# Moving the last subtraction of sixteen weight conversions from GpSimd to VectorE, and one conversion to the next step

## The chip, the cores and the metric

One core of a Trainium2 chip runs the whole program. Its engines work in parallel, each through its own queue in a fixed order: TensorE (PE in the profile; PEld is its weight load), VectorE (DVE), ScalarE (ACT), GpSimd (POOL) and SyncE (SP, which only issues transfers here). An instruction whose input is not ready holds back all that stand behind it on its engine. The metric is the device time of one execution, in microseconds; lower is better.

## The reference

Three layers follow one another: a decaying linear attention (2 batches, 8 heads, 768 positions, head size 64), a dense feed-forward layer with a gate, and a mixture of 8 experts of which each token takes one.

```python
x = attn_out.transpose(0, 2, 1, 3).reshape(B * S, H * D)          # 1536 x 512
h = x @ w_in                                                      # 512 x 2048
sp = np.where(h > 20.0, h, np.log1p(np.exp(np.minimum(h, 20.0))))
x = (h * np.tanh(sp)) @ w_out                                     # 2048 x 512
e_idx = np.argmax(x @ w_gate + modality_bias[modality_id], axis=1)
out[mask] = gate_w[mask, None] * (np.maximum(x[mask] @ w1[e], 0.0) @ w2[e])
```

`w_in` and `w_out` arrive as 64-bit floats. The kernel reads them as pairs of 32-bit words and makes of each weight a high and a low 32-bit part, so that a product is formed of three matmuls.

## The kernel before

The dense layer is cut into 16 blocks of 128 hidden columns (`fc`), and the 1536 tokens into 4 chunks of 384 (`c`). The list `order` (lines 865 and 866) sets the passes: first blocks 0 to 7 for chunks 0, 1 and 2, then blocks 8 to 15 for the same chunks, then all 16 blocks for chunk 3. A pass of the loop at line 867 is called a step here, and its number is `i`. Each step does four things:

- The first nine steps (0 to 8) carry the end of the attention (`attend`).
- `convert_next` takes one or two weight blocks from the list `wq`: it starts the transfer of the raw words (line 294 for `w_in`, 303 for `w_out`) and queues the conversion. There are 32 conversions; `stg["n"]` counts them. The first 16 are taken by step 5, the other 16 from step 9 on.
- `mm1` makes 12 matmuls for the step (line 804, into a PSUM tile `w`, of which there are three) and the gate: ScalarE line 809 (Exp), VectorE 810, ScalarE 811, 812, 813, VectorE 814, 815, 816, ScalarE 817, VectorE line 103 (`mg<-me,mg`). Line 816 is the last reader of the PSUM tile, so `mm1` of step i + 3 cannot start before line 816 of step i has ended.
- `mm2a` makes 9 matmuls (line 830) of the step three before, into three accumulators `a`, of which there are three. After blocks 0 to 7 of a chunk, `put_by` copies the accumulators out (ScalarE, line 386, into two halves of a tile `cv` and a tile `xq`) and writes them to DRAM (line 387). That is at steps 10, 18 and 26. The next chunk needs the three accumulators free.

A conversion (`convert`) is a chain over three engines: ScalarE 278 and 279, VectorE 280 and 281, ScalarE 282 (the high part), and GpSimd line 103 (the low part, `wo<-cv,wo` or `wi<-cv,wi`). Line 103 is the body of the helper `tt`, so it stands for many elementwise operations; the tile names tell them apart. From step 9 the raw words lie mostly in tile `cv`, which has two buffers in turn; a buffer is free when the low part of its conversion has been made. `put_by` takes its `cv` from the same two buffers.

The order of instructions on each engine is not that of the code: a scheduler in the build sorts them by its own estimate of when each is ready, and the order is then fixed.

Of the kernel before, what the change touches and what calls it, by code (L numbers as in the profile page):

```python
# [7 lines left out]
F32 = mybir.dt.float32  # L8
# [5 lines left out]
ALU = mybir.AluOpType  # L14
# [13 lines left out]
FA = 8  # L28
# [4 lines left out]
def tile_decay_attention_mish_moe_top1(  # L33
# [66 lines left out]
    V, A, G = nc.vector, nc.scalar, nc.gpsimd  # L100

    def tt(o, a, b, op, eng=None):
        (eng or V).tensor_tensor(out=o, in0=a, in1=b, op=op)  # L103
# [32 lines left out]
    n = 1  # L136
# [138 lines left out]
    def convert(raw, hi, lo):  # L275
        H_, L_ = raw[:, :, 1], raw[:, :, 0]
        hf = H_.bitcast(F32)
        A.activation(out=hf, in_=hf, func=AF.Copy, scale=REBIAS)  # L278
        A.activation(out=L_, in_=raw.rearrange("p f w -> p (f w)").bitcast(U8)[:, 3::8], func=AF.Copy, scale=2.0 ** -5, bias=2.0 ** -6 - 0.5)
        V.scalar_tensor_tensor(out=L_, in0=H_, scalar=-0x80000000, in1=L_, op0=ALU.bitwise_and, op1=ALU.bitwise_or)  # L280
        V.scalar_tensor_tensor(out=H_, in0=H_, scalar=3, in1=L_, op0=ALU.logical_shift_left, op1=ALU.bitwise_or)  # L281
        A.activation(out=hi, in_=hf, func=AF.Copy)
        tt(lo, hf, hi.bitcast(F32), ALU.subtract, G)

    stg = {"tags": ["cv", "cv"], "n": 0}

# [5 lines left out]
    def load_wi(fc):  # L292
        s = raw_tile()
        nc.sync.dma_start(out=s.rearrange("p (a f) w -> p a (f w)", a=KC),
                          in_=w_in[:, fc * 2 * P:(fc + 1) * 2 * P].rearrange("(a p) f -> p a f", p=P))
        t = T([P, 2, KC, P], F32R, f"wi{fc}")
        tf = t.rearrange("p h a f -> p h (a f)")
        convert(s, tf[:, 0], tf[:, 1])
        wi[fc] = t

    def load_wo(fc):
        s = raw_tile()
        nc.sync.dma_start(out=s.rearrange("p f w -> p (f w)"), in_=w_out[fc * P:(fc + 1) * P, :])
        t = T([P, 2, DM], F32R, f"wo{fc}")
        convert(s, t[:, 0], t[:, 1])
        wo[fc] = t
# [4 lines left out]
    def convert_next(n, limit=NFC):  # L311
        for _ in range(n):
            ok = [w for w in wq if w[2] < limit]
            if ok:
                wq.remove(ok[0])
                _, kind, f = ok[0]
                (load_wi if kind == "i" else load_wo)(f)
# [446 lines left out]
    def early(which, fc):  # L764
        if which == 1:
            if fc == 8:
                E2["R1"] = [T([P, FF], F32, f"wi{j}") for j in range(4)]
                E2["er"] = nc.sync.value_load(E2["e0"][0:1, 0:1], min_val=0, max_val=NE - 1)
                load_raw(E2["er"], 1)
            if 10 <= fc < 14:  # L770
                j = fc - 10
                E2["W1h"].append(T([P, FF], F32R, f"wi{4 + j}"))
                E2["W1l"].append(T([P, FF], F32R, f"wi{8 + j}"))
                split(E2["W1h"][j], E2["W1l"][j], E2["R1"][j])
            if fc == 14:
                E2["XTh"] = T([P, KC, 256], F32R, "wi12")
                E2["XTl"] = T([P, KC, 256], F32R, "wi13")
                prep_x(gather(E2["u"][0], (0, 1), NE1 * P), 2)
        else:
            if fc == 5:  # L780
                E2["R2"] = [T([P, 2, DM], F32, f"wo{j}") for j in range(4)]
                load_raw(E2["er"], 2)
            if 10 <= fc < 14:
                j = fc - 10
                E2["W2h"].append(T([P, 2, DM], F32R, f"wo{4 + j}"))
                E2["W2l"].append(T([P, 2, DM], F32R, f"wo{8 + j}"))
                split(E2["W2h"][j], E2["W2l"][j], E2["R2"][j])
# [3 lines left out]
    def step():  # L791
        if steps:
            f = steps.pop(0)
            if f is not None:
                f()

    def mm1(c, fc):
        ph = PS([P, CW], "w")
        n = 0
        for kk in range(KC):  # L800
            wh, wl = wi[fc][:, 0, kk, :], wi[fc][:, 1, kk, :]
            xh, xl = xth[c][:, kk, :], xtl[c][:, kk, :]
            for a_, b_ in ((wh, xh), (wh, xl), (wl, xh)):
                nc.tensor.matmul(ph, lhsT=a_, rhs=b_, start=(n == 0), stop=(n == 3 * KC - 1))  # L804
                n += 1
        ex = T([P, CW], F32, "me", 3)
        gg = T([P, 2, CW], F32R, "mg", 4)
        rr = T([P, CW], F32, "mr", 1)
        A.activation(out=ex, in_=ph, func=AF.Exp)  # L809
        V.tensor_scalar(out=ex, in0=ex, scalar1=EXP20, scalar2=None, op0=ALU.min)  # L810
        A.activation(out=ex, in_=ex, func=AF.Square, bias=one[:, 0:1])  # L811
        A.activation(out=rr, in_=ex, func=AF.Ln, bias=one[:, 0:1])  # L812
        A.activation(out=gg[:, 1], in_=rr, func=AF.Exp, scale=-1.0)  # L813
        V.scalar_tensor_tensor(out=ex, in0=ex, scalar=1.0, in1=gg[:, 1].bitcast(F32), op0=ALU.add, op1=ALU.mult)  # L814
        V.scalar_tensor_tensor(out=ex, in0=ex, scalar=-2.0, in1=gg[:, 1].bitcast(F32), op0=ALU.add, op1=ALU.mult)  # L815
        V.scalar_tensor_tensor(out=ex, in0=ex, scalar=0.5, in1=ph, op0=ALU.add, op1=ALU.mult)  # L816
        A.activation(out=gg[:, 0], in_=ex, func=AF.Copy)  # L817
        tt(gg[:, 1], ex, gg[:, 0].bitcast(F32), ALU.subtract)
        gs[c, fc] = gg

    def mm2a(c, fc):
        divided_at = FA if c < NCK - 1 else NFC
        if fc in (0, divided_at):
            accs[c] = [PS([P, DM], "a") for _ in range(CT)]
        gg = gs.pop((c, fc))
        wh, wl = wo[fc][:, 0], wo[fc][:, 1]
        for j in range(CT):
            gh, gl = gg[:, 0, j * P:(j + 1) * P], gg[:, 1, j * P:(j + 1) * P]
            for i, (a_, b_) in enumerate(((gh, wh), (gh, wl), (gl, wh))):
                nc.tensor.matmul(accs[c][j], lhsT=a_, rhs=b_, start=(fc in (0, divided_at) and i == 0),  # L830
                                 stop=(fc in (divided_at - 1, NFC - 1) and i == 2))
        if fc == divided_at - 1 < NFC - 1:
            put_by(c, accs.pop(c))
        if c < NCK - 1 and fc == NFC - 3:
            fetch(c)
        if c == NCK - 1:
            early(2, fc)
        if fc == NFC - 1:
            steps.extend(route(c, accs.pop(c)))
            if c == NCK - 2:  # L840
                steps.extend([stage1, stage1b, None, stage1c, lambda: slots(0, NE1)])

    def attend(it):
        if it + 2 < NIT:
            keys(it + 2)
        if it + 2 < NIT:
            queries(it + 2)
        if it + 3 < NIT:
            load_q(it + 3)
        if it == 0:  # L850
            decay(1, s1)
        elif it + 1 < NIT:
            decay(it + 1, scores(it + 1))
        if it + 3 < NIT:
            load_k(it + 3)
        combine(it)
        if it + 2 < NIT:
            load_v(it + 2)
# [8 lines left out]
    for i, (c, fc) in enumerate(order):  # L867
        it = CT + i
        if it < NIT:
            if it == NIT - CT:  # L870
                stg["tags"] = ["cv", "cv", "wi10"]
            attend(it)
            convert_next(2, FA)
        else:
            if it == NIT:
                stg["tags"] = ["cv", "wo14", "cv", "wo15"]
            if wq and wq[0][2] >= 13:
                stg["tags"] = ["cv", "cv"]
            convert_next(2 if i < FA + 1 or i % 3 == 0 else 1)
        mm1(c, fc)  # L880
        step()
        if c == NCK - 1:
            early(1, fc)
        if i >= LAG:
            mm2a(*order[i - LAG])
        step()
# [317 lines left out]
```

## Time and profile before

| | |
|---|---|
| median of three runs | 574.85 us (574.23 to 575.75) |
| profiled execution, its own time | 574.69 us |
| span of its instructions | 573.0 us |
| TensorE busy | 528.6 us (92%) |
| VectorE busy | 343.6 us (60%) |
| ScalarE busy | 302.3 us (53%) |
| GpSimd busy | 117.5 us (21%) |
| mean granted TensorE clock | 0.980 of full speed |

In the rows of the profile a timeline entry gives start, duration, engine, line, operation and tiles, and in brackets how long the engine stood idle before it and what ended the idle time. A table by stretch gives the stretch, its length, then busy time and count of TensorE matmul, TensorE weight load, VectorE, ScalarE and GpSimd, then the granted TensorE clock, the share of the transfer engines and GB/s. A row of a group gives the count, busy time in us, mean ns of one, and after the bar the idle time before them with its releasers. All starts are us from the start of the span.

### The profile page before, as it was taken

What the parts mean: (1) busy time and instruction counts of PE and PEld (TensorE: products, weight loads), DVE (VectorE), ACT (ScalarE), POOL (GpSimd) and SP (SyncE); (2) the same over time, 40 slices, a digit from 0 to 9 for tenths busy, and PEclk for the clock granted to TensorE, in tenths of its full rate; (3) what the DMA queues carried; (4) which work ended last, traced back from release to release, by engine and by line L of the source; (5) the groups of instructions that cost most, each with busy time, mean ns of one, the idle gap of its engine ahead of it and who ended that gap; (6) DMA issues with size and microseconds to landing.
All of it is one profiled execution on the core that took longest, in us unless ns stands there. A gap on an engine that the chain in (4) does not pass through costs nothing.

```text
span 573.0 us, 10275 instructions
## 1 busy us (share of the span) xinstructions
PE 528.6 (92%) x3577; PEld 457.7 (80%) x3578; DVE 343.6 (60%) x814; ACT 302.3 (53%) x580; POOL 117.5 (21%) x100
## 2 busy tenths in 40 slices
PE   7898989989979999999999999999788998998993
PEld 4687768778768889999998999989677887778882
DVE  3579989788887656766767599947512024503020
ACT  2457867778887766656566479632111124412120
POOL 1654453423321000000000003000502212312111
PEclk9999989999989999999999999999888999999998
DMA  8999565323342020011030046001469427402120
GB/s 161 235 249 266 139 151 148 112 92 112 110 128 112 19 92 1 0 44 67 1 94 17 2 152 234 2 0 57 116 226 350 149 58 254 156 28 69 49 59 34
DMA packets 67371, 62.24 MB, mean 109 GB/s; under 512 B 42183, under 2 KB 51919, under 8 KB 67280
## 3 DMA queue, kind: packets, MB, share of 16 engines
q1 hardware_dynamic: 62064, 51.65, 30.5%
q0 software_dynamic: 2976, 9.44, 5.5%
q8 instruction: 44, 0.72, 0.5%
q10 hardware_dynamic: 2240, 0.05, 0.2%
q14 instruction: 47, 0.39, 0.2%
HBM read 52.47 MB, written 8.86 MB: 107 GB/s over the span
## 4 chain that ended last, share of the span: by engine, by line
PE 41%; DMA 24%; issue 14%; DVE 7%; ACT 7%; POOL 5%; SPq 1%; POOLq 0%; DVEq 0%; ACTq 0%
PE a L830 16%; PE w L804 15%; DMA out_dram<-cv,xth 9%; DMA out_dram<-xth,xth 9%; DMA cv<-in_moe_w_out_dram 3%; POOL wo L103 3%; PE a L571 2%; PE w L581 2%; PE r L433 2%; DMA cv<-in_moe_w_in_dram 2%; POOL wi L103 1%; DVE cv L280 1%; DVE cv L281 1%; ACT cv L278 1%; DMA out_dram<-mg,xth 1%
## 5 line engine op out<-in xcount | busy, mean ns | idle before, releaser
L830 PE MATMUL a<-wo,mg 128*128 128x512 f32 x576 | 148.3, 399 | 5.4 <-ACT cv L386 2.8
L804 PE MATMUL w<-xth,wi 128*128 128x384 f32 x512 | 146.1, 345 | 3.6 <-DVE me L816 3.1
L830 PEld LDWEIGHTS a<-wo,mg 128*128 128x128 f32 x576 | 106.7, 189 | 27.5 <-ACT cv L386 4.0
L804 PEld LDWEIGHTS w<-xth,wi 128*128 128x128 f32 x512 | 94.5, 189 | 10.1 <-DVE me L816 5.7
L804 PE MATMUL w<-xtl,wi 128*128 128x384 f32 x256 | 86.8, 339 | 0.0
L581 PE MATMUL w<-wi,wi 128*128 128x256 f32 x576 | 75.4, 290 | 9.5 <-issue 7.6
L581 PEld LDWEIGHTS w<-wi,wi 128*128 128x128 f32 x576 | 72.9, 195 | 11.7 <-issue 9.0
L585 DVE SCALAR_TENSOR_TENSOR wo<-w,wi 128x256 fp32r<-128x256 f32 x48 | 20.2, 424 | 84.1 <-ACT wi L584 76.8
L571 PE MATMUL a<-wo,wi 128*128 128x512 f32 x192 | 62.5, 407 | 4.5 <-ACTq L1143 3.0
L814 DVE SCALAR_TENSOR_TENSOR me<-me,mg 128x384 f32<-128x384 f32 x64 | 41.5, 649 | 31.0 <-ACT mg L813 30.8
L804 PEld LDWEIGHTS w<-xtl,wi 128*128 128x128 f32 x256 | 48.6, 190 | 1.7
L584 ACT ACTIVATE wi<-w 128x256 fp32r<-128x256 f32 x48 | 18.2, 384 | 58.7 <-PE w L581 58.7
L817 ACT ACTIVATE mg<-me 128x384 fp32r<-128x384 f32 x64 | 33.3, 520 | 28.2 <-DVE me L816 27.8
L809 ACT ACTIVATE me<-w 128x384 f32<-128x384 f32 x64 | 31.0, 485 | 30.5 <-PE w L804 30.0
L571 PEld LDWEIGHTS a<-wo,wi 128*128 128x128 f32 x192 | 35.7, 192 | 13.7 <-issue 6.2
L811 ACT ACTIVATE me<-me,one 128x384 f32<-128x384 f32 x64 | 39.0, 609 | 12.0 <-DVE me L810 11.7
L103 DVE TENSOR_TENSOR mg<-me,mg 128x384 fp32r<-128x384 f32 x64 | 36.6, 573 | 10.6 <-ACT mg L817 10.2
L812 ACT ACTIVATE mr<-me,one 128x384 f32<-128x384 f32 x64 | 39.3, 613 | 1.2
L815 DVE SCALAR_TENSOR_TENSOR me<-me,mg 128x384 f32<-128x384 f32 x64 | 38.5, 602 | 1.1
L571 PE MATMUL a<-wo,wo 128*128 128x512 f32 x96 | 38.6, 402 | 0.0
L816 DVE SCALAR_TENSOR_TENSOR me<-me,w 128x384 f32<-128x384 f32 x64 | 35.2, 551 | 1.5
L103 POOL TENSOR_TENSOR xtl<-xtl,id 128x1152 f32<-128x1152 f32 x1 | 2.1, 2116 | 156.5 <-DVE xtl L103 156.5
(269 smaller groups left out, 724.7 us busy)
## 6 DMA issues: line engine op xcount, KB each, us to landing
xtl<-in_moe_w_dram SPq DMA_DIRECT2D x24, 256.0 KB
cv<-in_moe_w_out_dram SPq DMA_DIRECT2D x11, 512.0 KB
cv<-in_moe_w_in_dram SPq DMA_DIRECT2D x9, 512.0 KB
wi<-in_moe_w_dram SPq DMA_DIRECT2D x8, 512.0 KB
wo<-in_moe_w_dram SPq DMA_DIRECT2D x8, 512.0 KB
wo<-in_k_dram SPq DMA_DIRECT2D x12, 256.0 KB
wi<-in_q_dram SPq DMA_DIRECT2D x12, 256.0 KB
wo<-in_v_dram SPq DMA_DIRECT2D x12, 256.0 KB
```

The costliest lines, as they stand in the source:

```text
L103: (eng or V).tensor_tensor(out=o, in0=a, in1=b, op=op)
L571: nc.tensor.matmul(po, lhsT=a_, rhs=b_, start=(f == 0 and i == 0), stop=(f == FC2 - 1 and i == 2))
L581: nc.tensor.matmul(ph, lhsT=a_, rhs=b_, start=(n == 0), stop=(n == 3 * KC - 1))
L804: nc.tensor.matmul(ph, lhsT=a_, rhs=b_, start=(n == 0), stop=(n == 3 * KC - 1))
L809: A.activation(out=ex, in_=ph, func=AF.Exp)
L811: A.activation(out=ex, in_=ex, func=AF.Square, bias=one[:, 0:1])
L812: A.activation(out=rr, in_=ex, func=AF.Ln, bias=one[:, 0:1])
L814: V.scalar_tensor_tensor(out=ex, in0=ex, scalar=1.0, in1=gg[:, 1].bitcast(F32), op0=ALU.add, op1=ALU.mult)
L815: V.scalar_tensor_tensor(out=ex, in0=ex, scalar=-2.0, in1=gg[:, 1].bitcast(F32), op0=ALU.add, op1=ALU.mult)
L816: V.scalar_tensor_tensor(out=ex, in0=ex, scalar=0.5, in1=ph, op0=ALU.add, op1=ALU.mult)
L817: A.activation(out=gg[:, 0], in_=ex, func=AF.Copy)
L830: nc.tensor.matmul(accs[c][j], lhsT=a_, rhs=b_, start=(fc in (0, divided_at) and i == 0), stop=(fc in (divided_at - 1, NFC - 1) and i == 2))
```

## The change

`tt` gets its engine from the count of conversions: the first 16 keep GpSimd, the last 16 use VectorE. And of the steps whose number divides by three only those under 16 take two conversions.

```diff
         A.activation(out=hi, in_=hf, func=AF.Copy)
-        tt(lo, hf, hi.bitcast(F32), ALU.subtract, G)
+        tt(lo, hf, hi.bitcast(F32), ALU.subtract, G if stg["n"] <= 2 * FA else V)
...
-            convert_next(2 if i < FA + 1 or i % 3 == 0 else 1)
+            convert_next(2 if i < FA + 1 or (i % 3 == 0 and i < 2 * FA) else 1)
```

Step 18 is the first of them. There `convert_next` took blocks 12 and 13 of `w_out`, then block 14 at step 19 and block 15 at step 20; now it takes block 12 at step 18, 13 at 19, 14 at 20 and 15 at 21.

On VectorE, at the conversion of block 11 of `w_out` (raw words `cv_1650`, low part `wo11_1652`), with the gate of step 15 (`me_1628`), of step 16 (`me_1672`) and of step 17 (`me_1716`):

```order
+L103 TENSOR_TENSOR wi14_1608<-cv_1606,wi14_1608 128x512 [waits Activation_49]
 L815 SCALAR_TENSOR_TENSOR me_1628<-me_1628,mg_1629 128x384 [waits DVE_49]
-L810 TENSOR_SCALAR me_1672<-me_1672 128x384 [waits Activation_49]
+L280 SCALAR_TENSOR_TENSOR cv_1650<-cv_1650 128x512 [waits DMAHW2_49,Activation_49]
 L816 SCALAR_TENSOR_TENSOR me_1628<-me_1628,w_1615 128x384 [waits DVE_49]
-L280 SCALAR_TENSOR_TENSOR cv_1650<-cv_1650 128x512 [waits DMAHW2_49,Activation_49,Pool_49]
 L281 SCALAR_TENSOR_TENSOR cv_1650<-cv_1650 128x512 [waits DVE_49]
+L810 TENSOR_SCALAR me_1672<-me_1672 128x384
 L103 TENSOR_TENSOR mg_1629<-me_1628,mg_1629 128x384 [waits PE_49,Activation_49]
+L810 TENSOR_SCALAR me_1716<-me_1716 128x384
+L103 TENSOR_TENSOR wo11_1652<-cv_1650,wo11_1652 128x512 [waits Activation_49]
 L814 SCALAR_TENSOR_TENSOR me_1672<-me_1672,mg_1673 128x384 [waits Activation_49]
```

The low parts now stand among the gates, line 810 of step 16 stands behind lines 280 and 281 of the raw words instead of ahead of them, and line 810 of step 17 stands ahead of line 814 of step 16.

On ScalarE, at the write-out of chunk 1 (`put_by` at step 18), before the change; `cv_1747` holds the raw words of block 13 of `w_out`, `cv_1791` and `xq_1792` are the tiles of the write-out, `me_1769` is the gate of step 18:

```order
L386 ACTIVATE xq_1792<-a_1446 128x512 [waits DMAHW5_49,PE_49]
L811 ACTIVATE me_1769<-me_1769,one_169 128x384 [waits DVE_49]
L812 ACTIVATE mr_1771<-me_1769,one_169 128x384 [waits Activation_49]
L282 ACTIVATE wo12_1740<-cv_1738 128x512 [waits DVE_49]
L813 ACTIVATE mg_1770<-mr_1771 128x384 [waits Activation_49]
L278 ACTIVATE cv_1747<-cv_1747 128x512 [waits DMAHW5_49,Pool_49]
L279 ACTIVATE cv_1747<-cv_1747 128x512
L386 ACTIVATE cv_1791<-a_1444 128x512 [waits Pool_49]
L386 ACTIVATE cv_1791<-a_1445 128x512
```

The same place after the change, where the gate of step 18 is `me_1760` and the tiles of the write-out are `cv_1782` and `xq_1783`:

```order
L386 ACTIVATE xq_1783<-a_1446 128x512 [waits DMAHW5_49,PE_49]
L278 ACTIVATE cv_1738<-cv_1738 128x512 [waits DMAHW4_49,DVE_49]
L282 ACTIVATE wi15_1696<-cv_1694 128x512 [waits DVE_49]
L817 ACTIVATE mg_1673<-me_1672 128x384 [waits DVE_49]
L279 ACTIVATE cv_1738<-cv_1738 128x512
L811 ACTIVATE me_1760<-me_1760,one_169 128x384 [waits DVE_49]
L386 ACTIVATE cv_1782<-a_1444 128x512 [waits DVE_49]
L812 ACTIVATE mr_1762<-me_1760,one_169 128x384 [waits Activation_49]
L386 ACTIVATE cv_1782<-a_1445 128x512
```

The copies into `cv` waited for the low part of block 12 of `w_out` and stood behind lines 278 and 279 of block 13; now they wait for the low part of block 15 of `w_in`, one conversion earlier in the turn of the two buffers, and block 13 comes after them.

On SyncE, at the same place, before the change (`cv_1747` and `cv_1799` are blocks 13 and 14 of `w_out`):

```order
L303 DMA cv_1738<-in_moe_w_out_dram 128x1024 [waits DMAHW2_49,Pool_49]
L303 DMA cv_1747<-in_moe_w_out_dram 128x1024 [waits DMAHW5_49,DMAHW3_49,Pool_49]
L387 DMA part_231<-xq_1792 128x512 [waits Activation_49]
L387 DMA part_231<-cv_1791 128x512 [waits Activation_49] x2
L303 DMA cv_1799<-in_moe_w_out_dram 128x1024 [waits DMAHW5_49,Pool_49]
```

And after it (`cv_1790` and `cv_1837` are blocks 13 and 14):

```order
L303 DMA cv_1738<-in_moe_w_out_dram 128x1024 [waits DMAHW2_49,DVE_49]
L387 DMA part_231<-xq_1783 128x512 [waits DMAHW5_49,Activation_49]
L387 DMA part_231<-cv_1782 128x512 [waits Activation_49] x2
L303 DMA cv_1790<-in_moe_w_out_dram 128x1024 [waits DMAHW4_49,DVE_49]
L303 DMA cv_1837<-in_moe_w_out_dram 128x1024 [waits DMAHW7_49,DMAHW6_49,DMAHW3_49]
```

The transfer of block 13 moves behind the three writes of the write-out. Every transfer of raw words waited for GpSimd's low part of the buffer's last user and now waits for VectorE's. On GpSimd 16 rows go and none comes; its next work after the attention is then a single row, at 344.76 us in the trace of before.

## Rows read from the trace of the kernel before

**Rows 1.** Table by stretch, core 0, 112 to 190 us and within it.

```profile
112.00:190.00 78.00, 69.28 (x327) 59.16 (x326) 63.06 (x104) 63.92 (x125) 22.73 (x16) 0.98 0.33 108
...
130.00:165.00 35.00, 32.43 (x160) 27.96 (x158) 30.04 (x51) 29.86 (x58) 11.19 (x7) 1.00 0.35 112
```

**Rows 2.** Timeline of TensorE, 110 to 192 us: groups that waited.

```profile
114.90 0.44 PE L804 MATMUL w<-xth,wi 128*128 128x384 f32 x1 [0.29 <-DVE xtl L103]
...
128.19 1.87 PE L830 MATMUL a<-wo,mg 128*128 128x512 f32 x6 [1.58 <-ACT cv L386]
...
157.26 0.44 PE L804 MATMUL w<-xth,wi 128*128 128x384 f32 x1 [1.18 <-DVE me L816]
...
167.35 1.18 PE L830 MATMUL a<-wo,mg 128*128 128x512 f32 x3 [2.54 <-ACT xq L386]
...
168.32 0.52 PE L804 MATMUL w<-xth,wi 128*128 128x384 f32 x1
...
172.67 1.64 PE L830 MATMUL a<-wo,mg 128*128 128x512 f32 x6 [1.26 <-ACT cv L386]
...
190.11 0.44 PE L804 MATMUL w<-xth,wi 128*128 128x384 f32 x1 [0.76 <-DVE me L816]
```

**Rows 3.** Chain that ended last, two of its undisturbed TensorE pieces.

```profile
194.54 2.10 PE w L804 x12
...
236.62 2.09 PE w L804 x12
```

**Rows 4.** Table by stretch again, 168 to 170 us.

```profile
168.00:170.00 2.00, 2.00 (x8) 1.90 (x7) 0.76 (x3) 1.91 (x4) 0.39 (x1) 0.50 0.71 186
```

**Rows 5.** Timeline of VectorE and GpSimd, 119 to 123 us.

```profile
119.16 3.07 POOL L103 TENSOR_TENSOR wi<-wo,wi 128x512 fp32r<-128x512 f32 x2 [5.33 <-ACT wi L282]
...
119.53 1.52 DVE L814 SCALAR_TENSOR_TENSOR me<-me,mg 128x384 f32<-128x384 f32 x1
120.98 1.47 DVE L810 TENSOR_SCALAR me<-me 128x384 f32<-128x384 f32 x1
```

**Rows 6.** Groups of VectorE instructions, shapes apart, 112 to 190 us.

```profile
L814 DVE SCALAR_TENSOR_TENSOR me<-me,mg 128x384 f32<-128x384 f32 x16 | 12.4, 777 | 7.2 <-ACT mg L813 7.1
...
L810 DVE TENSOR_SCALAR me<-me 128x384 f32<-128x384 f32 x15 | 10.1, 673 | 0.9 <-ACT me L809 0.9
...
L815 DVE SCALAR_TENSOR_TENSOR me<-me,mg 128x384 f32<-128x384 f32 x15 | 9.4, 629 | 0.3
...
L816 DVE SCALAR_TENSOR_TENSOR me<-me,w 128x384 f32<-128x384 f32 x15 | 8.2, 549 | 0.3
```

**Rows 7.** The same groups where GpSimd is silent, 200 to 236 us.

```profile
L814 DVE SCALAR_TENSOR_TENSOR me<-me,mg 128x384 f32<-128x384 f32 x9 | 5.0, 559 | 11.1 <-ACT mg L813 11.1
...
L816 DVE SCALAR_TENSOR_TENSOR me<-me,w 128x384 f32<-128x384 f32 x9 | 5.0, 554 | 0.3
...
L810 DVE TENSOR_SCALAR me<-me 128x384 f32<-128x384 f32 x9 | 3.2, 352 | 0.0
```

**Rows 8.** Instructions on tile cv, 107 to 200 us: duration min/median/max.

```profile
L281 DVE SCALAR_TENSOR_TENSOR cv<-cv x13: 680/685/695, 109.8 to 185.2; 128x512 int32<-128x512 int32 x13
...
L103 POOL TENSOR_TENSOR wo<-cv,wo x8: 1306/1360/1862, 134.5 to 186.9; 128x512 fp32r<-128x512 f32 x8
```

**Rows 9.** Groups of ScalarE instructions, shapes apart, 112 to 190 us.

```profile
L811 ACT ACTIVATE me<-me,one 128x384 f32<-128x384 f32 x15 | 9.2, 611 | 6.8 <-DVE me L810 6.8
...
L278 ACT ACTIVATE cv<-cv 128x512 f32<-128x512 f32 x11 | 7.4, 677 | 4.3 <-DMA cv<-in_moe_w_out_dram 2.7 <-POOL wo L103 1.0 <-DMA cv<-in_moe_w_in_dram 0.7
...
L282 ACT ACTIVATE wo<-cv 128x512 fp32r<-128x512 f32 x8 | 5.4, 671 | 0.4 <-DVE cv L281 0.3
```

**Rows 10.** Timeline of ScalarE around the second write-out of accumulators.

```profile
170.91 0.69 ACT L278 ACTIVATE cv<-cv 128x512 f32<-128x512 f32 x1 [0.96 <-POOL wo L103]
...
172.04 1.05 ACT L386 ACTIVATE cv<-a 128x512 f32<-128x512 f32 x2
```

**Rows 11.** Chain that ended last: one load of raw weights.

```profile
152.22 3.32 DMA cv<-in_moe_w_out_dram
```

## The prediction

> **What bounds the kernel now.** The page puts TensorE first, so I asked where it stands still. The table by stretch shows it busy for 69.28 of the 78 us from 112 to 190 [rows 1]: the steps that carry the last 16 conversions. The timeline of TensorE then shows what ended each wait [rows 2]: twice ScalarE's copies of accumulators (1.58 us, then 2.54 and 1.26 in one write-out), and several times VectorE's line 816, which gives the PSUM tile of three steps earlier back (1.18, 0.76). TensorE also loses time at half speed. After the 2.54 us wait the granted clock was 0.50 from 168 to 170 us [rows 4], the lower of its two levels (1.2 of 2.4 GHz), and the nine matmuls that begin at 168.32 last until 171.41 (172.67 less its wait of 1.26), 3.1 us, where nine of an undisturbed twelve take 9/12 x 2.10 = 1.6 [rows 2, 3]: 1.5 us lost.
>
> How much can be had: `mm1` of step 9 starts at 114.90 and that of step 24 at 190.11 [rows 2], 75.2 us for 15 steps. In the chain, ten undisturbed steps lie between 194.54 and 236.62 [rows 3], 4.21 us each, so 15 would take 63.1. Lost: 12.1 us, and 0.29 ahead of step 9, together 12.4. Behind step 24 TensorE waits for next to nothing until the experts, whose work hangs on these steps as before; so what is won here is won at the end, and no more than 12.4 us.
>
> **Why VectorE is late.** From 119.16 GpSimd makes two low parts in 3.07 us, and in just that time VectorE's line 814 takes 1.52 us and line 810 1.47 [rows 5]. Where GpSimd is silent they take 0.56 and 0.35 [rows 7]. Over the stretch, line 814 averages 777 ns, 810 673 and 815 629 [rows 6], against 559, 352 and (815 has the form of 814) 559 [rows 7]. Excess: 16 x 0.218 + 15 x 0.321 + 15 x 0.070 = 9.4 us. Line 816, whose second input is in PSUM, averages 549 against 554 [rows 6, 7]: not stretched.
>
> The Trainium skill (SBUF — State Buffer, Who interferes with whom) has a rule for this: VectorE instructions with two SBUF inputs, or in a two-port mode, and GpSimd instructions that read SBUF shut each other out for a whole instruction, while an instruction with one SBUF input is left alone. The trace agrees, line 816 included (549 ns). By this rule the whole excess goes once GpSimd is silent, and the sum is that of the forecast; without it, it would be that of the third rival below.
>
> **The change part by part.**
>
> *Sixteen low parts on VectorE.* The trace has no such subtraction from `cv` on VectorE. The nearest row is line 281, 128x512 with two SBUF inputs, 0.685 us, against 1.36 on GpSimd [rows 8]. Starts of successive independent rows lie some 0.08 closer than durations (119.53 to 120.98 is 1.45 of 1.52 [rows 5]), so a low part holds VectorE 0.60: 16 x 0.60 = 9.6 us. Bounds: 0.56, the time of the 384-wide line 814, from below, GpSimd's own 1.36 from above; I take line 281's for its size. Against the 9.4 us of relief VectorE's load stays as it was, but the two do not fall in the same place: the relief is on lines 810, 814 and 815, which stand on the way to line 816, and the low part is on nobody's way except that of its buffer.
>
> *The buffer comes free sooner*, by 1.36 - 0.685 = 0.68 us and the wait for GpSimd's queue, but the next transfer takes 3.3 us [rows 11] and in-order VectorE may be elsewhere. I give this nothing by itself.
>
> *The orders.* I carried the starts forward by hand along the new orders from 111 us on: each row begins when its engine is free and its releaser has ended, with the durations of rows 6 to 9 (ScalarE 0.61 for line 811, 0.68 for 278, 0.67 for 282, starts 0.1 closer), 3.3 to 3.8 us for a transfer, and 4.2 for an undisturbed step.
> - *Steps 9 to 12.* Lines 814 and 810 of 119.53 and 120.98 give 2 us back, the gate of step 10 is earlier, and the second copy of chunk 0's write-out ends at 124.9 instead of 128.1. The waits of 0.29 and 1.58 vanish [rows 2]. `mm1` of step 12 ends at 129.6 instead of 132: 2.4 us won.
> - *Steps 13 to 18.* Line 816 arrives 2.0, 1.3 and 0.3 us ahead of need for three of these, and 0.45 late for step 17. The waits of this stretch (1.18 before step 18) go; 4.1 us won by step 18.
> - *Step 19* is where the new order costs. Line 810 of step 16 is ready at 148.5, but stands behind lines 280 and 281 of block 11, whose raw words land at 150.2 (buffer free 146.8, 3.4 for the transfer); ScalarE's two conversions end at 151.65, VectorE's 280, 816 and 281 at 153.4, line 810 at 153.7. Lines 282, 811 twice, 812, 278 and 813 on ScalarE take until 156.65, and line 816 of step 16, with 280 and 281 of the next block among its rows, ends at 159.4. `mm2a` has ended at 157.35: TensorE waits 2.1 us, more than before at this place; 3.0 us won by step 19.
> - *Second write-out.* Before, the copies into `cv` began at 172.04, behind lines 278 (170.91, itself waiting for GpSimd) and 279 of block 13 [rows 10]. Now that block comes after. The first copy is done at 159.0, the others at 162.1 and 163.1, just as TensorE asks for them. The 2.54, the 1.26 and the half-speed stretch go.
> - *Block 13's transfer* goes behind three writes on SyncE. Its buffer is free at 165.65, after these; it lands at 169.1 and ScalarE takes it at 169.4. Block 15, now last, is ready at 182.4. Its weights are not wanted until step 34, so the later place costs nothing; without that cover each late conversion would cost its transfer, 3.3 us.
> - *Steps 20 to 24* then pass with 0.4 to 2 us to spare, and `mm1` of step 24 starts at 180.65.
>
> **The sum.** 190.11 - 180.65 = 9.5 us won; what remains of the 12.4 is the 2.1 and 0.45 us of waits and trifles. The profiled execution took 574.69 (span 573.0, 1.7 around it): 574.69 - 9.5 = 565.2. A wait of 2.1 us at step 19 may or may not be followed by half speed, as that of 2.54 was (three matmuls of line 830 in 1.18 us) and that of 1.58 was not (six in 1.87) [rows 2]; I add half of 1.5: 566.0. The median of the runs is 0.16 above the profiled execution; I say 566.1.
>
> **The rivals.**
> - *ScalarE paces, not VectorE.* ScalarE is busy 29.86 of the 35 us from 130 to 165, VectorE 30.04 [rows 1], and the change takes nothing from ScalarE. For: it has no slack for being late. Against: its longest waits are for line 810 (6.8 us [rows 9]). Then the wait of step 19 recurs twice more among steps 17 to 23, 2 x 2.1 us: 566.1 + 4.2 = 570.3.
> - *The wait only changes its place.* If every later pair of steps with a conversion (16 and 17, 18 and 19, 20 and 21, 22 and 23) costs 2.1 us and for two of them the half speed of 1.5, 11.4 us are lost of the 12.4 that are lost now: 573.8, no change. For: line 810 of two steps stand together ahead of line 814 of the first at these places. Against: the margins above.
> - *VectorE becomes the bound, slower.* If the long rows do not come from GpSimd, nothing is given back and 9.6 us are added on an engine that is idle for 5 of 35 us [rows 1]: seven low parts of that stretch are 4.2 us, which leaves it 0.8. The low parts then delay line 816 by as much, less the 5.3 us (2.54 + 1.26 + 1.5) of the second write-out: 574.85 + 9.6 - 5.3 = 579.2. It decides from a relief under 4.3 us (of the 9.4) on. Against: rows 5, where long rows and GpSimd coincide.
>
> The Trainium skill (Perfetto Trace Analysis, Optimizing Scalar/DVE Operations) advises giving work to GpSimd when VectorE is saturated, which is what this change takes back, and so points to the last rival; the same place adds that moving work between these two may not help because of the read port they share. The trace agrees with the second half (1.52 against 0.56 us).
>
> **How the numbers follow.** Forecast 0.62, ScalarE paces 0.22, wait moves 0.07, VectorE bound 0.09. The likeliest case by itself spans 562.5 (574.85 - 12.4, every loss gone) to 568.5; taking GpSimd's 1.36 for a low part as upper bound adds 16 x 0.68 = 10.8 us to VectorE's load and leads to the third rival. The range reaches into the first rival to 571.0. Runs of this kernel can tell a change from none beyond about 0.3%, 1.7 us: faster 0.84, same 0.07, slower 0.09.
>
> **What would show it.** Right: lines 810 and 814 near 0.35 and 0.56 us between 112 and 185; no wait for line 386 above 0.5 us near 160 to 165; granted clock 1.0 there, or a short dip after the one wait of some 2 us; `mm1` of step 24 near 181; VectorE's busy time within 3 us of before; nothing changed behind step 24 but the start. Wrong: waits of TensorE for line 816 at several steps between 150 and 185, with line 811 on ScalarE waiting for 810, or low parts on VectorE near 1 us.

## The result: 566.03 us, against 575.3 us before

| | before | after |
|---|---|---|
| median of the runs beside each other | 575.3 us (6 runs, 570.96 to 577.62) | 566.03 us (6 runs, 564.78 to 567.89) |
| ratio, 95% interval | | 0.9843 [0.9817, 0.987] |
| profiled execution | 574.69 us, span 573.0 | 564.78 us, span 563.1 |
| `mm1` of step 9, of step 24 begins at | 114.90, 190.11 | 113.16, 180.63 |
| steps 9 to 24 | 75.2 us | 67.5 us |
| span behind the start of step 24 | 382.9 us | 382.5 us |

The forecast was 566.1 us. In the profiled executions the change is worth 574.69 - 564.78 = 9.91 us: 7.74 us between step 9 and step 24 (75.21 - 67.47), 1.74 us ahead of step 9 and 0.4 behind step 24, as the spans have it.

The medians here and below are of all runs; the ratios leave out the few that were more than 1.5% above the fastest of their kernel.

The table of busy times and three groups of the page of the changed kernel (busy, mean of one; idle time before them and its releaser):

```profile
PE 521.4 (93%) x3577; PEld 455.0 (81%) x3578; DVE 342.7 (61%) x830; ACT 301.2 (53%) x580; POOL 94.9 (17%) x84
...
L804 PE MATMUL w<-xth,wi 128*128 128x384 f32 x512 | 145.6, 344 | 2.3 <-DVE me L816 2.1
L830 PE MATMUL a<-wo,mg 128*128 128x512 f32 x576 | 146.4, 396 | 0.2 <-ACT xq L386 0.2
...
L814 DVE SCALAR_TENSOR_TENSOR me<-me,mg 128x384 f32<-128x384 f32 x64 | 37.9, 593 | 26.1 <-ACT mg L813 25.9
```

VectorE has 16 instructions more than before and is busy for 342.7 us, where it was 343.6: what it does more it gets back elsewhere. TensorE's line 830 waited for 0.2 us in all.

The table by stretch (busy time of TensorE, its loads, VectorE, ScalarE, GpSimd; then granted clock, DMA share, GB/s) shows the steps that [rows 1] showed, and two stretches of 2 us in which TensorE was granted 0.59 and 0.55 of its clock, so that it ran for most of them at half speed, as in [rows 4]:

```profile
112.00:190.00 78.00, 75.63 (x369) 67.42 (x368) 66.71 (x132) 68.08 (x136) 0.00 (x0) 0.98 0.33 105
130.00:165.00 35.00, 32.88 (x157) 29.35 (x156) 31.94 (x63) 31.19 (x62) 0.00 (x0) 0.95 0.35 114
158.00:160.00 2.00, 1.93 (x7) 1.93 (x8) 2.00 (x6) 2.00 (x5) 0.00 (x0) 0.59 0.34 131
160.00:162.00 2.00, 2.00 (x8) 2.00 (x7) 1.97 (x4) 2.00 (x6) 0.00 (x0) 0.55 0.29 109
```

TensorE is busy for 75.63 of the 78 us, 6.35 more than before. The timeline of TensorE names every group that waited between 107 and 200 us; there are three, where [rows 2] had waits of 1.58, 2.54 and 1.26 for line 386 and 1.18 and 0.76 for line 816:

```profile
113.16 0.33 PE L804 MATMUL w<-xth,wi 128*128 128x384 f32 x1
...
125.44 0.98 PE L830 MATMUL a<-wo,mg 128*128 128x512 f32 x3 [0.25 <-ACT xq L386]
...
147.58 0.45 PE L804 MATMUL w<-xth,wi 128*128 128x384 f32 x1 [0.23 <-DVE me L816]
...
158.07 0.45 PE L804 MATMUL w<-xth,wi 128*128 128x384 f32 x1 [1.90 <-DVE me L816]
...
180.63 0.44 PE L804 MATMUL w<-xth,wi 128*128 128x384 f32 x1
```

The groups of VectorE's instructions, shapes apart, 112 to 190 us, which answer to [rows 6]:

```profile
L814 DVE SCALAR_TENSOR_TENSOR me<-me,mg 128x384 f32<-128x384 f32 x18 | 10.0, 555 | 5.6 <-ACT mg L813 5.5
L815 DVE SCALAR_TENSOR_TENSOR me<-me,mg 128x384 f32<-128x384 f32 x18 | 10.0, 554 | 0.2
L816 DVE SCALAR_TENSOR_TENSOR me<-me,w 128x384 f32<-128x384 f32 x18 | 9.9, 549 | 0.1
...
L810 DVE TENSOR_SCALAR me<-me 128x384 f32<-128x384 f32 x18 | 6.4, 354 | 2.2 <-ACT me L809 2.2
L103 DVE TENSOR_TENSOR wo<-cv,wo 128x512 fp32r<-128x512 f32 x8 | 5.5, 686 | 0.8 <-ACT wo L282 0.8
```

Lines 814, 810 and 815 went from 777, 673 and 629 ns to 555, 354 and 554; line 816, which was not stretched, stayed at 549. A low part takes 686 ns. ScalarE's line 811 waited for line 810 for 1.7 us in this stretch, where [rows 9] had 6.8:

```profile
L811 ACT ACTIVATE me<-me,one 128x384 f32<-128x384 f32 x18 | 10.6, 607 | 1.8 <-DVE me L810 1.7
```

### The profile page after: what moved, and what is told of

It is laid out like the page before. It is cut to its first block, busy times and chain, and to the rows that moved or that the text cites. A ratio compares the mean times of both kernels' runs of the same rounds, so it can differ in the third digit from the quotient of the medians.

```text
span 563.1 us, 10255 instructions
## 1 busy us (share of the span) xinstructions
PE 521.4 (93%) x3577; PEld 455.0 (81%) x3578; DVE 342.7 (61%) x830; ACT 301.2 (53%) x580; POOL 94.9 (17%) x84
## 4 chain that ended last, share of the span: by engine, by line
PE 45%; DMA 21%; issue 12%; ACT 8%; DVE 8%; POOL 3%; POOLq 1%; SPq 1%; another core or an unknown queue 0%; DVEq 0%; ACTq 0%
PE a L830 18%; PE w L804 18%; DMA out_dram<-cv,xth 8%; DMA out_dram<-xth,xth 8%; PE w L581 2%; PE r L433 2%; DMA cv<-in_moe_w_in_dram 2%; DMA cv<-in_moe_w_out_dram 1%; DMA out_dram<-mg,xth 1%; POOL wo L103 1%; DVE cv L280 1%; ACT cv L278 1%; PE r L426 1%; ACT me L811 1%; ACT cv L279 1%
## 5 line engine op out<-in xcount | busy, mean ns | idle before, releaser
L830 PE MATMUL a<-wo,mg 128*128 128x512 f32 x576 | 146.4, 396 | 0.2 <-ACT xq L386 0.2
L581 PE MATMUL w<-wi,wi 128*128 128x256 f32 x576 | 74.0, 287 | 9.7 <-issue 4.9
L581 PEld LDWEIGHTS w<-wi,wi 128*128 128x128 f32 x576 | 71.6, 192 | 11.9 <-issue 5.9
L571 PE MATMUL a<-wo,wi 128*128 128x512 f32 x192 | 62.5, 407 | 4.5 <-ACTq L1143 3.1
L814 DVE SCALAR_TENSOR_TENSOR me<-me,mg 128x384 f32<-128x384 f32 x64 | 37.9, 593 | 26.1 <-ACT mg L813 25.9
L815 DVE SCALAR_TENSOR_TENSOR me<-me,mg 128x384 f32<-128x384 f32 x64 | 37.4, 585 | 1.0
```

The lines of the kernel that those rows point to most:

```text
L571: nc.tensor.matmul(po, lhsT=a_, rhs=b_, start=(f == 0 and i == 0), stop=(f == FC2 - 1 and i == 2))
```

## The experiments

Each was timed in five rounds beside the kernel before, in three batches in which the kernel before had medians of 575.24, 576.31 and 575.09 us; across batches the ratios compare better than the medians. A run's total also scatters by what lies far from the change: in the profiled executions of these kernels the span behind step 24 is between 379.8 and 388.7 us, with no order among them. So the table gives the stretch from the start of `mm1` of step 9 to that of step 24 as well, from one profile each; undisturbed it would be 63.1 us by the prediction's reckoning, which is some 0.6 too high: the best kernel of the table took 62.5.

| kernel | median us | ratio to before, 95% | steps 9 to 24 |
|---|---|---|---|
| before | 575.3 | | 75.2 |
| the change | 566.03 | 0.9843 [0.9817, 0.987] | 67.5 |
| engine alone | 567.18 | 0.9855 [0.9815, 0.9895] | 67.5 |
| move alone | 574.96 | 0.9995 [0.9965, 1.0025] | 75.1 |
| change, 13 useless 128x512 on GpSimd | 574.1 | 0.9981 [0.9954, 1.0008] | 73.8 |
| change, 13 useless 128x16 on GpSimd | 567.13 | 0.9857 [0.9824, 0.989] | 65.9 |
| the same with 13 memsets | 567.16 | 0.9847 [0.9798, 0.9896] | 67.6 |
| change, buffers held on GpSimd | 567.71 | 0.9853 [0.9814, 0.9892] | 69.0 |
| before, one conversion a step | 575.55 | 1.0005 [0.9983, 1.0027] | 75.2 |
| change, one a step from step 10 | 563.32 | 0.9787 [0.9735, 0.984] | 63.2 |
| change, one a step from step 9 | 565.32 | 0.9826 [0.9791, 0.9862] | 65.2 |
| change, all 32 low parts on VectorE | 564.3 | 0.9821 [0.9774, 0.9868] | 66.4 |
| all 32 on VectorE, one a step from step 10 | 560.31 | 0.9752 [0.973, 0.9775] | 62.5 |

My theory: GpSimd, while it reads SBUF, holds up VectorE's instructions that want the same, and the gain is the end of that. Rivals: the moved conversion makes the gain; the sooner turn of the raw buffers makes it; the conversions stand too close together, whatever engine makes the low parts.

### The two parts apart

Engine alone, as a change to the changed kernel:

```diff
-            convert_next(2 if i < FA + 1 or (i % 3 == 0 and i < 2 * FA) else 1)
+            convert_next(2 if i < FA + 1 or i % 3 == 0 else 1)
```

> The engine part alone: the last 16 low parts on VectorE, and block 13 of w_out again converted at step 18 instead of 19. My theory (GpSimd's reads of SBUF stretch the gate's rows, and the move only frees the second write-out's buffers): lines 810 and 814 stay near 0.35 and 0.56 us, the steps up to 17 run as in the changed kernel, and at the second write-out, where the copies into cv stand again behind lines 278 and 279 of block 13, one or two waits of TensorE for line 386 return, 2 to 3.8 us with what half speed follows: 569.5 us (568 to 571.5). If the engine does it all and the move is nothing: 566.0. If the move does it all: 575.

Move alone:

```diff
-        tt(lo, hf, hi.bitcast(F32), ALU.subtract, G if stg["n"] <= 2 * FA else V)
+        tt(lo, hf, hi.bitcast(F32), ALU.subtract, G)
```

> The move alone: all low parts on GpSimd as before, block 13 of w_out converted at step 19. My theory: lines 810 and 814 stay stretched (averages near 0.67 and 0.78 us between 112 and 190), the wait of 1.6 us at the first write-out and those for line 816 stay, and only the second write-out's 2.54 + 1.26 us and its half speed can go: 571 us (569.5 to 573). If the move does it all: 566. If it is nothing by itself, because the low part of GpSimd comes too late for the copies all the same: 575.

Measured: 567.18 and 574.96 us. The engine makes the gain; the move makes none that can be told from nothing, alone or on top (567.18 against 566.03, with intervals that overlap). Both of my expectations gave the move 2 to 4 us too many. With the engine alone the copies into `cv` do stand behind lines 278 and 279 of block 13. ScalarE's and TensorE's timelines of that kernel:

```profile
165.01 0.66 ACT L278 ACTIVATE cv<-cv 128x512 f32<-128x512 f32 x1
165.56 0.67 ACT L279 ACTIVATE cv<-cv 128x512 int32<-128x512 uint8 x1
166.13 1.07 ACT L386 ACTIVATE cv<-a 128x512 f32<-128x512 f32 x2
```

```profile
165.73 0.33 PE L804 MATMUL w<-xth,wi 128*128 128x384 f32 x1
165.90 3.89 PE L830 MATMUL a<-wo,mg 128*128 128x512 f32 x15
```

The copies end at 167.2, and TensorE ran its 15 matmuls through without a wait in the record. In the written order the accumulator that `xq` had freed takes three matmuls of the next step ahead of those that need `cv`; that covers the copies. With the move alone the copies stand ahead of block 13, and TensorE waits all the same (timelines of GpSimd, ScalarE and TensorE):

```profile
164.42 1.30 POOL L103 TENSOR_TENSOR wi<-cv,wi 128x512 fp32r<-128x512 f32 x1 [4.83 <-ACT wi L282]
```

```profile
165.75 0.60 ACT L386 ACTIVATE cv<-a 128x512 f32<-128x512 f32 x1
```

```profile
166.41 1.07 PE L830 MATMUL a<-wo,mg 128*128 128x512 f32 x3 [2.66 <-ACT cv L386]
```

The copy begins when GpSimd's low part of block 15 of `w_in` has ended, and that began late because the high part ahead of it was late. Lines 814 and 810 average 799 and 582 ns in this kernel.

### GpSimd's reading put back

The changed kernel, with one useless GpSimd instruction for each of the first 13 of the last 16 blocks; it reads the high part twice, and its result goes to a tile that nobody reads. It holds no raw buffer, and only one row has to wait for it: the high part of block 13 of `w_out`, whose tile it borrows. That row began at 179.57 us, 6 us after the last of the 13 had ended:

```diff
+    def extra(hi, hf): d = stg.setdefault("d", stg.get("d") or T([P, 1024], F32, "wo13")) if stg["n"] > 2 * FA and len(wo) < 13 else None; d is None or G.tensor_tensor(out=d[:, 0:512], in0=hi.bitcast(F32)[:, 0:512], in1=hi.bitcast(F32)[:, 0:512], op=ALU.subtract)
```

> The changed kernel, and on GpSimd 13 useless subtractions of 128x512, one for each of the first 13 of the last 16 blocks: both inputs are the block's high part, the result goes to a tile that nobody reads, so that GpSimd reads SBUF as before but no buffer is held for it and nobody waits for it. My theory: 13 of the 16 long pairs return, lines 810 and 814 average above 0.6 and 0.7 us, and since VectorE also has its low parts now the gates are late at several steps: 574 us (571 to 579, the third rival of the prediction). If the gain came from the sooner turn of the buffers, or from dropping the wait for GpSimd's queue: as the changed kernel, 566.

The control has `0:16` in place of `0:512` three times:

> As the kernel with 13 useless subtractions on GpSimd, but each only 128x16: the same instructions, order and semaphores with next to no reading. My theory: 566 us (565 to 567.5), lines 810 and 814 near 0.35 and 0.56. If the presence of the instruction or its semaphores costs: as that kernel, 574.

Measured: 574.1 and 567.13 us. An instruction on whose result nothing depends takes back 7.0 us, against 9.3 that the change won with all 16 blocks, and the same instruction with next to no reading takes back nothing that can be told. The low parts stay on VectorE in both, so the first is not the kernel before again; it shows that the reading by itself costs about as much as the change won. Of the groups of VectorE's instructions, 112 to 190 us, two lines of the first kernel and then the same two of the control:

```profile
L815 DVE SCALAR_TENSOR_TENSOR me<-me,mg 128x384 f32<-128x384 f32 x16 | 12.2, 762 | 0.2
L810 DVE TENSOR_SCALAR me<-me 128x384 f32<-128x384 f32 x16 | 6.8, 426 | 0.3 <-ACT me L809 0.3
```

```profile
L815 DVE SCALAR_TENSOR_TENSOR me<-me,mg 128x384 f32<-128x384 f32 x19 | 10.6, 556 | 0.2
L810 DVE TENSOR_SCALAR me<-me 128x384 f32<-128x384 f32 x18 | 6.3, 353 | 0.6 <-ACT me L809 0.6
```

GpSimd's and VectorE's timelines of the first kernel show how:

```profile
150.19 1.48 POOL L284 TENSOR_TENSOR wo<-wo 128x512 f32<-128x512 f32 x1 [4.07 <-ACT wo L282]
155.20 1.59 POOL L284 TENSOR_TENSOR wo<-wi 128x512 f32<-128x512 f32 x1 [3.52 <-ACT wi L282]
159.74 1.04 POOL L284 TENSOR_TENSOR wo<-wo 128x512 f32<-128x512 f32 x1 [2.95 <-ACT wo L282]
```

```profile
150.69 1.40 DVE L814 SCALAR_TENSOR_TENSOR me<-me,mg 128x384 f32<-128x384 f32 x1
152.12 0.56 DVE L815 SCALAR_TENSOR_TENSOR me<-me,mg 128x384 f32<-128x384 f32 x1
...
155.21 0.68 DVE L103 TENSOR_TENSOR wi<-cv,wi 128x512 fp32r<-128x512 f32 x1
155.81 1.39 DVE L815 SCALAR_TENSOR_TENSOR me<-me,mg 128x384 f32<-128x384 f32 x1
```

GpSimd's 1.48 us end at 151.67, and line 814, issued at 150.69, ends 0.42 us later, where it takes 0.56 alone: most of its work came behind GpSimd's end. From 155.2 VectorE's low part passes in its own 0.68 while GpSimd's instruction becomes longer: 1.59 us, where the shortest of its kind took 1.04. Line 815 behind the low part then pays, until 0.41 us behind GpSimd's end. So either engine may be the one that waits. Which line of VectorE pays depends on which comes next (815 averages 762 ns, 814 604, 810 426).

### Is it the reading?

To the control, behind each 128x16 subtraction, a memset of GpSimd over the whole tile, which writes SBUF for 0.96 us and reads nothing:

```diff
+... and None or G.memset(d, 0.0)
```

> As the kernel with 13 subtractions of 128x16 on GpSimd, and behind each of them on GpSimd a memset of 128x1024, so that GpSimd is as long at work on SBUF as with the subtractions of 128x512, but reads nothing in that time. My theory, that it is GpSimd's reading that stretches VectorE's rows: lines 810 and 814 stay near 0.35 and 0.56 us, 567 us (565 to 569). If writing does the same: rows stretched as with the subtractions of 128x512, 572 to 575.

Measured: 567.16 us. GpSimd's rows and VectorE's rows in their time:

```profile
120.48 0.96 POOL L284 MEMSET wo<- 128x1024 f32 x1
...
123.44 0.96 POOL L284 MEMSET wo<- 128x1024 f32 x1
...
147.90 0.96 POOL L284 MEMSET wo<- 128x1024 f32 x1
```

```profile
120.76 0.89 DVE L810 TENSOR_SCALAR me<-me 128x384 f32<-128x384 f32 x1
...
123.63 0.98 DVE L810 TENSOR_SCALAR me<-me 128x384 f32<-128x384 f32 x1 [0.32 <-ACT me L809]
...
148.29 0.56 DVE L815 SCALAR_TENSOR_TENSOR me<-me,mg 128x384 f32<-128x384 f32 x1
```

Half of my expectation fell: line 810, which has one input and runs 384 columns in 0.35 us, was stretched by writing too, both times that it began well inside a memset (its average is 416 ns). Lines 814 and 815, with two inputs in SBUF, were not (554 and 557). The Trainium skill (SBUF — State Buffer, Who interferes with whom) says just this: two SBUF inputs collide with GpSimd's reading alone, an instruction in a two-port mode with anything that GpSimd does there. These rows agree in both halves if line 810 runs in such a mode; its 0.35 us, against 0.55 for the lines beside it, suggests so, but no row names the mode.

The medians do not tell this kernel from its control (567.16 and 567.13). The stretch does in one profile each: 67.6 us against 65.9, at a granted clock of 1.00 in both, with a wait of 1.01 us for line 386 behind the two long rows where the control had 0.28. So writing is not free either, but it did not bring back what reading did (73.8).

### The turn of the buffers

The control with a second 128x16 subtraction that reads the raw words, so that each of those 13 buffers comes back nearly as late as before the change:

```diff
+... and None or G.tensor_tensor(out=d[:, 16:32], in0=hf[:, 0:16], in1=hi.bitcast(F32)[:, 0:16], op=ALU.subtract)
```

> The changed kernel with two subtractions of 128x16 on GpSimd for each of the first 13 blocks, the second of which reads the block's raw words: together they last about as long as GpSimd's low part did, 1.3 us, so that the buffer is given back as late as before the change, while next to nothing is read. My theory (the sooner turn of the buffers is worth nothing or little): lines 810 and 814 unstretched, 567 us (565 to 568.5). If the turn of the buffers makes the gain: 571 to 575.

Measured: 567.71 us. A pair of them in GpSimd's timeline, which gives the buffer back 1.15 us after it began (146.25 to 147.40), the middle value of the 13; GpSimd's low parts of `w_out` had taken 1.36 [rows 8]:

```profile
146.25 0.65 POOL L284 TENSOR_TENSOR wo<-wo 128x16 f32<-128x16 f32 x1 [4.04 <-ACT wo L282]
146.87 0.53 POOL L284 TENSOR_TENSOR wo<-cv,wo 128x16 f32<-128x16 f32 x1
```

By the medians the hold costs 1.7 us against the changed kernel (567.71 - 566.03) and 0.6 against its control (567.13), and the intervals do not tell either from nothing. The stretch is 1.5 us longer than that of the change (69.0 and 67.5, with half speed in both). So the sooner turn of the buffers may be a part of the gain, but is not the most of it.

### Fewer conversions in a step

On the kernel before and on the changed kernel, steps 12 and 15 (in the kernel before step 18 too) take one conversion instead of two:

```diff
+            convert_next(2 if i < FA + 2 else 1)
```

> The kernel before, all low parts on GpSimd, with one conversion a step from step 10 on. My theory (VectorE's rows stay stretched, so that with fewer conversions in a step some of the gates come in time but not all): lines 810 and 814 near 0.6 and 0.75 us, waits of TensorE left at the write-outs, 571 us (568 to 573). If the crowding of the conversions was the whole trouble and the engine none: 564.

> The changed kernel with one conversion a step from step 10 on (steps 12 and 15 take one instead of two, so that the last block is converted at step 23, not 21). My theory: what is left of the loss, the wait of 1.9 us at step 19 for line 816, comes from the rows of two conversions that stand ahead of the gates there; with one a step it goes, and with it the half speed behind it, 15 steps in about 64 us instead of 67.5: 563.5 us (562 to 565.5). If the wait only moves to a later step: 566. If later conversions make mm1 wait for its weights: above 567.

Measured: 575.55 and 563.32 us. With GpSimd at work the spreading is worth nothing: lines 814 and 810 average 848 and 631 ns, and at the second write-out TensorE waits for 1.41 and 2.22 us. My 571 was too low. Once GpSimd is silent, spreading takes away what the change had left of the stretch; the median is 2.7 us lower than the change's, with intervals that overlap. The only wait that TensorE's timeline names there from 107 to 190 us:

```profile
126.26 0.96 PE L830 MATMUL a<-wo,mg 128*128 128x512 f32 x3 [0.21 <-ACT xq L386]
```

Steps 9 to 24 took 63.15 us (114.02 to 177.17). Step 9 with one conversion as well (`convert_next(1)`):

> As the kernel with one conversion a step from step 10 on, and step 9 takes one too (last block at step 24). My theory: the same as that kernel or a little better, 563.5 us (562 to 565.5). If later conversions make mm1 wait for its weights, of which those of block 8 of w_in are wanted from step 24 on: above 567.

Measured: 565.32 us, with a wait of 0.52 for line 386 and one of 1.57 for line 816 at step 23. `mm1` did not wait for weights, so neither of the two cases I had written down is what happened. The chain that ended last shows what did: a block of `w_in` could be loaded into its `cv` buffer only when the second write-out had left it (163.28), its transfer took 4.28 us, and ScalarE's line 278 stood waiting for it until 167.74, ahead of line 811 of a gate, whose line 816 then came at 173.76.

### All 32 low parts on VectorE

```diff
-        tt(lo, hf, hi.bitcast(F32), ALU.subtract, G if stg["n"] <= 2 * FA else V)
+        tt(lo, hf, hi.bitcast(F32), ALU.subtract, V)
```

> The changed kernel with the low parts of all 32 blocks on VectorE, those made during the attention too. My theory (VectorE gets back from the stretched rows about what a low part costs it): VectorE's busy time as a whole stays within 3 us, and the attention ends at about the same time; 566 us (563 to 569). If VectorE's load grows by the whole 16 x 0.6 us in the attention, where it is busy for 8 to 9 tenths: 575.

And with it one conversion a step from step 10 on:

> Both at once on the changed kernel: the low parts of all 32 blocks on VectorE, and one conversion a step from step 10 on. My theory (the first gains some 2 us in the attention, the second takes away what waits are left in steps 9 to 24): steps 9 to 24 in about 63.5 us, 561.5 us (559.5 to 563.5). If the two gains are one and the same: 564.

Measured: 564.3 and 560.31 us. VectorE's busy time on the page is 344.4 us in the first, 1.7 more than in the changed kernel, for 16 x 0.686 = 11.0 us of low parts: again nearly all comes back. Step 9 begins at 111.21 and 112.28; in the other profiled kernels between 112.62 and 114.90, in one profile each. The interval of the first overlaps the change's. The second has the best time of all, and its interval lies clear of the change's. The page's busy times of the second, and its steps 9 and 24 in TensorE's timeline:

```profile
PE 524.5 (94%) x3577; PEld 458.1 (82%) x3578; DVE 344.7 (62%) x846; ACT 301.8 (54%) x580; POOL 69.8 (13%) x68
```

```profile
112.28 0.33 PE L804 MATMUL w<-xth,wi 128*128 128x384 f32 x1
...
174.80 0.33 PE L804 MATMUL w<-xth,wi 128*128 128x384 f32 x1
```

## Why the prediction was right, and where it was not

**Relief of 9.4 us against a cost of 9.6.** Right in mechanism and size: the lines came down to 555, 354 and 554 ns, a low part took 0.686 us, and VectorE's busy time moved by 0.9 us. That GpSimd's reading costs this much was shown by putting it back alone (574.1 us) and by its control (567.13).

**Steps 9 to 12, and 13 to 18.** 2.4 and 4.1 us won were forecast by step 12 and step 18. Measured from step 9 on, with the 0.29 ahead of it: step 12 begins 13.09 us behind step 9 instead of 14.99, 1.9 + 0.29 = 2.2 us; step 18 begins 38.71 behind it instead of 42.36, 3.9 us. Step 17 was to be 0.45 late and was 0.23.

**Step 19.** The forecast wait of 2.1 us was 1.90, for the reason given. VectorE's timeline of the changed kernel has line 810 of step 16 behind lines 280 and 281 of block 11, and the same kind of rows ahead of its line 816:

```profile
151.30 0.69 DVE L281 SCALAR_TENSOR_TENSOR cv<-cv 128x512 int32<-128x512 int32 x1
151.90 0.35 DVE L810 TENSOR_SCALAR me<-me 128x384 f32<-128x384 f32 x1
...
155.22 0.56 DVE L814 SCALAR_TENSOR_TENSOR me<-me,mg 128x384 f32<-128x384 f32 x1 [1.63 <-ACT mg L813]
...
157.47 0.55 DVE L816 SCALAR_TENSOR_TENSOR me<-me,w 128x384 f32<-128x384 f32 x1
```

**The half speed behind that wait** was the term that was off in size within the stretch: 0.75 us stood for it. The chain that ended last has the twelve matmuls of step 19 at 3.91 us, where an undisturbed twelve take 2.10 [rows 3]:

```profile
158.07 3.91 PE w L804 x12
```

That is 1.8 us. The walk had 180.65 - 114.61 = 66.0 us for the 15 steps behind step 9, with no half speed in it; 67.5 were measured.

**`mm1` of step 24 at 180.65** was met (180.63), but partly by luck. The profiled execution began step 9 1.74 us sooner, and it began step 8 already 1.29 us sooner (108.85 against 110.14), before either kernel makes the first of the 16 low parts. The other kernels that keep the first 16 on GpSimd began step 8 between 108.32 and 110.24, without an order. The rest, 0.45 us, holds the wait of 0.29 that the change removed. So the change's own part is 7.74 + 0.45 = 8.2 us, where 9.5 were forecast, or 8.75 with the half speed allowed for.

**The second write-out** is where the reasoning failed without costing a number. I had the 2.54 and 1.26 us and the half speed go because block 13 comes after the copies. They went, but the move alone leaves a wait of 2.66 there, and without the move there is none. What takes them away is the engine; that it does so because VectorE's rows, ScalarE's high part and the low part behind it all come sooner is read from the timelines, not tried by itself.

**The buffer that comes free sooner** was given nothing, and the held buffers show 0.6 to 1.7 us, not told from nothing. **Block 13's later place** was given nothing, and that held.

**The rivals.** "ScalarE paces" (two more waits of 2.1 us) did not come; nor did "the wait only changes its place". "VectorE becomes the bound" was tried in effect, by the kernel with both GpSimd's reading and the low parts on VectorE: 574.1 us with 13 of 16 blocks, not the 579.2 worked out for all, so its price looks too high, and the outcome would have been "no change".

## What to carry to other kernels

Work given to GpSimd to relieve VectorE is not free for VectorE when both read SBUF at the same time: look for VectorE groups whose mean is far above the same group's in a stretch where GpSimd is silent, multiply, and compare with what the work would cost on VectorE itself. Here the two were equal (9.4 and 9.6 us), and taking it back still gained 1.6%: the stretched rows stood on the way to TensorE's buffers, and the low parts did not, as the last kernel shows, which has all of them on VectorE and ran steps 9 to 24 in 62.5 us without a wait of TensorE. Spreading such work over more steps paid only after the collision was gone (in steps 9 to 24 nothing before and 4.3 us after; by the medians 2.7, with overlapping intervals, and 4.0 with all 32 low parts on VectorE), so the order of two edits can decide whether the second seems worthless.

## What the runs showed that I had not expected

A wait of TensorE of about 2 us in these steps was sometimes followed by the lower of its two clock levels and sometimes not. In the profiles of the change, the engine alone and the held buffers, waits of 1.90, 1.89 and 2.26 us were (granted 0.59, 0.50 and 0.51 in a stretch of 2 us at or just behind the end of the wait). With the tiny subtractions, the memsets and all 32 on VectorE, waits of 1.74, 1.82 and 2.08 us were not (1.00), nor were the three of 1.85 to 2.18 us with GpSimd's reading put back. What decides it stays open.

GpSimd seems to pay too: its subtraction of 128x16, in the control, took 0.21 us at the least and 0.65 in the median, and the subtraction of 128x512 1.04 at the least and 1.48 in the median. The difference, 0.44 us in both, is less than one row of VectorE.
